# Steps 20 to 34 of a fused attention and ELU network with every engine's order written out and the weight conversion taken apart by engine

## The chip, the cores and the metric

The kernel runs on one core of one Trainium2 chip. The metric is the device time of one execution in microseconds, the median of several executions. The engines are named as in the profile: PE is TensorE, PEld its weight loads, DVE is VectorE, ACT ScalarE, POOL GpSimd, SP SyncE.

## The reference

A threshold attention over 8 sequences with 8 heads of 576 positions is followed by a two-layer network with an ELU between. The weights arrive as 64-bit floats. The reference, abridged:

```python
scores = scale * np.matmul(q, k.transpose(0, 1, 3, 2))
thresh = np.max(scores, axis=-1, keepdims=True) - tau
scores = np.where(scores >= thresh, scores, -1000000000.0)
attn = np.exp(scores - np.max(scores, axis=-1, keepdims=True))
attn = attn / (np.sum(attn, axis=-1, keepdims=True) + 1e-09)
x = np.matmul(attn, v)            # then (B, H, S, D) -> (B*S, H*D) = (4608, 512)
h = x @ w_in                      # (512, 2048)
g = np.where(h > 0.0, h, np.exp(np.minimum(h, 0.0)) - 1.0)
return g @ w_out                  # (2048, 512)
```

## The kernel before

The attention goes in 160 steps. Five steps make a pair of heads: four with two heads and 128 query rows, and one (called one-head here) with the last 64 rows of both. A step has scores on PE, a maximum over them on DVE, the bias and the threshold on POOL (`nb`, `th`), two exponentials on ACT, two masks with sums on DVE, a normalisation on POOL, and a turn of the weights, which PE does in steps 20 to 34 and DVE with DMA from 35 on. Units of the second network are put between: a unit is 8 matmuls of 128x256 or 4 of 128x512, and runs as two halves.

The double weights are turned to fp32 in 32 pieces of 128x512, 26 of them in steps 20 to 34. One piece, as it was:

```python
def convert_w():
    i = progress[1]
    ...
    top = wstage.tile([P, WN], U32, name="wtop", bufs=1)
    nc.vector.tensor_scalar(top, hi, 3, 0x3FFFFFFF, ALU.logical_shift_left, ALU.bitwise_and)      # L135
    nc.vector.scalar_tensor_tensor(top, hi, 0xC0000000, top, ALU.bitwise_and, ALU.bitwise_or)     # L136
    rest = lo.bitcast(I32)
    nc.scalar.mul(rest, lo, 2.0**-29)                                                              # L139
    top = top.bitcast(I32)
    nc.gpsimd.tensor_tensor(top, top, rest, ALU.add)                                               # L141
    mag = hi.bitcast(FP32)
    nc.scalar.activation(mag, mag, AF.Abs)                                                         # L144
    nc.vector.scalar_tensor_tensor(dst, mag, 1.125 * 2.0**-15, top.bitcast(FP32), ALU.is_ge, ALU.mult)  # L145
    load_w()
```

The loop of steps 20 to 34, whose order on the engines was left to the scheduler, and the quotas of the loop after it:

```python
for n in range(per_seq, SWITCH):          # 20 to 34
    pr, i = steps[n]
    ahead(pr, i)
    begin(pr, i, heads_of(i))             # scores, maximum, nb, th, exponentials
    convert_w()
    convert_w()
    finish(pr, i, heads_of(i))            # masks, normalisation
    turn(*steps[n - 1])
    behind(*steps[n - 2])                 # values
    due = min(due + rate, len(units))     # rate 1.4
    while due >= 1 and units:
        run_unit()
        due -= 1
...
# inside a unit of the first layer, and likewise of the second:
while progress[1] < 2 * KJ * (u // 4 + 1):
    convert_w()
...
QUOTA = ((2, 2), (2, 2), (2, 0), (2, 1), (2, 0))   # half units in each step of a pair, from step 35
```

## Time and profile before

| | before |
|---|---|
| device time, median of 4 | 1440.14 us (1438.64 to 1443.88) |
| first maximum with two heads, step 20 | at 105.8 us |
| step 20 to step 35, between their maxima | 159.1 us |
| step 35 to step 40 | 36.5 us |
| step 40 to the end of the span | 1134.6 us |

The last three rows are differences of start times of the maximum over the scores, which DVE takes once a step, so they cut the span at the same work in every kernel. A row of the timeline gives the start, the duration, the engine, the line, the operation, output and inputs, the shapes, and in brackets how long the engine had been idle and what ended that. The prediction shows the lines of before.

### The profile page before, as it was taken

How to read it: one execution, taken by the hardware profiler on the slowest of the kernel's cores; microseconds unless marked ns; L12 is line 12 of the kernel's file. 1: busy time of each engine (PE TensorE's matmuls, PEld its weight loads, DVE VectorE, ACT ScalarE, POOL GpSimd, SP SyncE). 2: the span in 40 equal slices, each digit the busy share in tenths (PEclk: the TensorE clock that was granted, in tenths of full speed). 3: DMA queues.
4: the chain of work that ended last, by engine and by line, in shares of the span. 5: the costliest groups of instructions: out<-in, count | busy, mean ns of one | idle time of the engine just before them, and what ended most of it. 6: DMA issues, size and time to landing. Idle time of an engine off the chain costs nothing.

```text
span 1436.0 us, 20455 instructions
## 1 busy us (share of the span) xinstructions
PE 1377.6 (96%) x6758; PEld 1023.8 (71%) x6758; DVE 949.1 (66%) x2070; ACT 451.2 (31%) x812; POOL 660.6 (46%) x1170
## 2 busy tenths in 40 slices
PE   6988788999999999999999999999999999999998
PEld 4555544647777777777777777777777777788887
DVE  6887665567677667766776767676777677563542
ACT  5665554323232222323232323232322222130220
POOL 4665554446544453536362635354444535151230
PEclk9999999999999999999999999999999999999999
DMA  4344443176667676767676767667676765100001
GB/s 95 78 92 113 111 125 93 43 196 191 188 171 207 178 191 173 193 186 190 178 192 186 189 180 193 185 183 201 180 199 174 191 189 166 62 1 15 15 1 30
DMA packets 298905, 205.45 MB, mean 143 GB/s; under 512 B 206384, under 2 KB 270384, under 8 KB 298800
## 3 DMA queue, kind: packets, MB, share of 16 engines
q1 hardware_dynamic: 298800, 204.15, 53.1%
q8 instruction: 54, 0.88, 0.2%
q14 instruction: 51, 0.42, 0.1%
HBM read 119.87 MB, written 84.21 MB: 142 GB/s over the span
## 4 chain that ended last, share of the span: by engine, by line
PE 82%; DVE 8%; POOL 4%; ACT 3%; issue 2%; DMA 1%; SPq 0%; POOLq 0%; DVEq 0%
PE ph L393 26%; PE po L500 24%; PE sc L220 12%; PE pv L347 8%; PE po L766 7%; DVE w L247 2%; PE pv L343 2%; PE po L465 2%; ACT e L235 2%; DVE mx L230 2%; POOL wtop L141 2%; PE rt L259 1%; POOL w L256 1%; DVE wtop L136 1%; POOL nb L231 1%
## 5 line engine op out<-in xcount | busy, mean ns | idle before, releaser
L393 PE MATMUL ph<-xt,w_in_sb 128*128 128x256 f32 x1792 | 409.3, 383 | 3.2 <-DVE w_in_sb L145 3.2
L393 PEld LDWEIGHTS ph<-xt,w_in_sb 128*128 128x128 f32 x1792 | 335.3, 190 | 70.2 <-issue 21.0
L235 ACT ACTIVATE e<-sc,nb,keep 128x576 f32<-128x576 f32 x288 | 227.8, 829 | 439.4 <-POOL nb L231 438.3
L230 DVE TENSOR_REDUCE mx<-sc 128x2 f32<-128x1152 f32 (+1 forms) x176 | 199.8, 1136 | 228.2 <-PE sc L220 228.0
L256 POOL TENSOR_SCALAR w<-w,rs 128x576 f32<-128x576 f32 x288 | 220.3, 775 | 223.3 <-DVE rs L250 216.6
L247 DVE SCALAR_TENSOR_TENSOR w<-sc,th,e 128x576 f32<-128x576 f32 x288 | 226.7, 815 | 78.0 <-ACT e L235 52.1
L220 PE MATMUL sc<-kT,qT 64*128 64x288 f32 x1024 | 180.4, 438 | 19.7 <-DVE w L247 9.6
L307 DVE STREAM_TRANSPOSE x<-w 128x512 f32<-128x512 f32 (+1 forms) x350 | 181.1, 567 | 0.9 <-POOL w L256 0.9
L231 POOL TENSOR_SCALAR nb<-mx,nkeep 128x2 f32<-128x2 f32 (+1 forms) x176 | 52.1, 296 | 263.4 <-DVE mx L230 256.5
L220 PEld LDWEIGHTS sc<-kT,qT 64*128 64x128 f32 x1024 | 99.3, 190 | 86.8 <-issue 53.5
L500 PE MATMUL po<-t,s 128*128 128x256 f32 x512 | 122.8, 386 | 4.5 <-DVE u L520 4.5
L500 PE MATMUL po<-w_out_sb,s 128*128 128x256 f32 x512 | 120.1, 384 | 0.0
L500 PEld LDWEIGHTS po<-t,s 128*128 128x128 f32 x512 | 94.6, 190 | 28.9 <-DVE u L520 8.9
L500 PEld LDWEIGHTS po<-w_out_sb,s 128*128 128x128 f32 x512 | 95.4, 190 | 19.7 <-issue 4.7
L401 ACT ACTIVATE g<-ph 128x512 f32<-128x512 f32 x112 | 66.9, 597 | 130.5 <-PE ph L393 130.5
L500 PE MATMUL po<-w_out_sb,g 128*128 128x256 f32 x448 | 103.2, 379 | 0.0
L404 POOL TENSOR_SCALAR g<-g 128x512 f32<-128x512 f32 x112 | 70.3, 627 | 67.4 <-ACT g L401 66.3
L500 PEld LDWEIGHTS po<-w_out_sb,g 128*128 128x128 f32 x448 | 85.1, 190 | 12.2
L408 DVE SCALAR_TENSOR_TENSOR g<-g,ph 128x512 f32<-128x512 f32 x112 | 75.0, 670 | 18.0 <-POOL g L404 17.9
L430 POOL TENSOR_TENSOR s<-g 128x256 f32<-128x256 f32 x112 | 82.6, 738 | 3.9 <-DVE g L810 3.9
L347 PE MATMUL pv<-wTb,vm 128*64 128x320 f32 x512 | 76.7, 439 | 0.0
L350 ACT COPY xt<-pv 128x256 f32<-128x256 f32 x64 | 23.8, 372 | 158.8 <-PE pv L347 158.8
(161 smaller groups left out, 1509.7 us busy)
## 6 DMA issues: line engine op xcount, KB each, us to landing
there<-x SPq DMA_DIRECT2D x500, 144.0 KB, 3.6
wTb<-there SPq DMA_DIRECT2D x75, 576.0 KB, 4.4
wTa<-there SPq DMA_DIRECT2D x50, 576.0 KB, 3.7
qm<-in_q_dram SPq DMA_DIRECT2D x128, 72.0 KB, 2.7
km<-in_k_dram SPq DMA_DIRECT2D x128, 72.0 KB, 3.7
vm<-in_v_dram SPq DMA_DIRECT2D x64, 128.0 KB, 2.5
wst<-in_moe_w_in_dram SPq DMA_DIRECT2D x16, 512.0 KB, 4.2
wst<-in_moe_w_out_dram SPq DMA_DIRECT2D x16, 512.0 KB, 3.7
```

The lines of the kernel that those rows point to most:

```text
L220: nc.tensor.matmul(scs[h][:, a, :HALF], qs[r], kT[r, k0 : k0 + HALF], start=True, stop=True)
L230: nc.vector.tensor_reduce(st["mx"][:, cs], src[:, :, :, :HALF], axis=AX.XY, op=ALU.max)
L235: nc.scalar.activation(e, st[h][:, :, :HALF], AF.Exp, bias=st["nb"][:, h : h + 1], scale=keep)
L247: nc.vector.scalar_tensor_tensor(wv, sc[:, :, :HALF], st["th"][:, h : h + 1], e, ALU.is_ge, ALU.mult, accum_out=sm[:, h : h + 1])
L256: nc.gpsimd.tensor_scalar(wv, wv, st["rs"][:, h : h + 1], 1.0, ALU.mult, ALU.mult)
L307: nc.vector.transpose(x[:, :, c0 : c0 + nc_], src.rearrange("p (c g n) -> p g c n", c=nc_, n=T))
L347: nc.tensor.matmul(pv[h * D : (h + 1) * D, g0 * T : g1 * T], vm[:, h, c], wT[:, g0:g1, h * (NC + 1) + c], start=False, stop=(c == NC - 1), ...
L393: nc.tensor.matmul(loc["ph"][:, k], w_in_sb[:, j, ft * P : (ft + 1) * P], xts[g][:, j, hf * CT : (hf + 1) * CT], start=(j == 0), stop=(j = ...
L408: nc.vector.scalar_tensor_tensor(loc["g"], loc["g"], 0.0, loc["h"], ALU.min, ALU.max)
L430: engines[k].tensor_tensor(out, x, y, op)
L500: nc.tensor.matmul(cur[c, place], lhs, rhs, start=(begins and u == 0), stop=(u == NU - 1), skip_group_check=True)
L766: nc.tensor.matmul(place, left[:, k], right[:, k], start=(begins and k == 0), stop=(k == 1), skip_group_check=True)
```

## The change

The intent is to keep DVE from standing inside each conversion. The five parts of a conversion become functions of their own and are laid at different places of a step; steps 20 to 34 get a written order on all engines; units start only when their weights are ready (`needs`); the weights of the first layer are converted in the order of their columns, and a unit of it takes two neighbouring column blocks (not in the cut below); the two output tiles of the second layer take turns, so that its weights are needed half as fast; and four half units more go into steps 35 to 39.

```diff
-    pieces = [(moe_w_in, ..., j, n) for n in (0, 2 * WN, WN, 3 * WN) for j in range(KJ)]
+    pieces = [(moe_w_in, ..., j, n) for n in range(0, DF, WN) for j in range(KJ)]
-        st = staged[i] = wstage.tile([P, WN, 2], U32, name="wst")
+        st = staged[i] = wstage.tile([P, WN, 2], U32, name="wst", bufs=4)
+    def convert_rest(i): ...   # ACT
+    def convert_top(i): ...    # DVE, two instructions; wtop with bufs=2
+    def convert_add(i): ...    # POOL
+    def convert_abs(i): ...    # ACT
+    def convert_end(i): ...    # DVE
...
-                units.extend((ffn2_plain, (c, i, p)) for i in range(2) for p in range(NFT // 4))
+                units.extend((ffn2_plain, (c, i, p)) for p in range(NFT // 4) for i in range(2))
...
+    SHARES = ((2, 1, 1), (1, 1, 0), (2, 1, 0), (1, 1, 0), (2, 1, 0))
+    with tc.manual_schedule():
+        for n in range(per_seq, SWITCH):
+            now = range(progress[1], min(progress[1] + 2, len(pieces)))
+            scores(*step, hs)
+            if valued: out_values = values(...)          # PE part only
+            for x in now[:1]: convert_top(x)
+            finish_units(carried, slice(0, 2))
+            for x in now[:1]: convert_add(x)
+            copies = parts[0]()
+            exponentials(*step, hs)                       # maximum, nb, th, exponentials
+            finish_units(carried, slice(2, None))
+            if valued: out_values(); copies()
+            for x in now[:1]: convert_abs(x)
+            after = ffn_halves(share[0])
+            for x in now[1:]: convert_top(x); convert_add(x); convert_abs(x)
+            ...                                           # turns, more halves
+            masks(*step, hs)
+            for x in now: convert_end(x)
+            finish_units(after + second, slice(2, None))  # ELU
+            normalize(*step, hs)
+            ...                                           # q, k, loads
+            for x in (the next two): convert_rest(x)
...
     QUOTA = ((2, 2), (2, 2), (2, 0), (2, 1), (2, 0))
+    FIRST = ((2, 2), (2, 2), (2, 2), (2, 2), (2, 1))      # for steps 35 to 39
```

(The loop is abridged: some `if`s stand on one line, and copies, shares and loads are cut.)

More of the change, by code (lines that the diff above doesn't have):

```diff
@@ L104, with load_w @@
     WN = 512
-    pieces = [(moe_w_in, w_in_sb[:, j, n : n + WN], j, n) for n in (0, 2 * WN, WN, 3 * WN) for j in range(KJ)]
+    pieces = [(moe_w_in, w_in_sb[:, j, n : n + WN], j, n) for n in range(0, DF, WN) for j in range(KJ)]
     pieces += [(moe_w_out, w_out_sb[:, f, n : n + WN], f, n) for f in range(NFT) for n in range(0, DM, WN)]
-    staged = {}
+    staged, tops = {}, {}
     progress = [0, 0]
-    def load_w():
+    def load_w(ahead=2):
         i = progress[0]
-        if i >= len(pieces) or i >= progress[1] + 2:
+        if i >= len(pieces) or i >= progress[1] + ahead:
             return
@@ L119, in load_w, with convert_rest, convert_top, convert_add @@
             return
-        st = staged[i] = wstage.tile([P, WN, 2], U32, name="wst")
+        st = staged[i] = wstage.tile([P, WN, 2], U32, name="wst", bufs=4)
         nc.sync.dma_start(st.rearrange("p n w -> p (n w)"), rows.bitcast(U32)[:, 2 * n : 2 * (n + WN)])
+    def convert_rest(i):
+        if i in staged:
+            lo = staged[i][:, :, 0]
+            nc.scalar.mul(lo.bitcast(I32), lo, 2.0**-29)
+    def convert_top(i):
+        if i in staged:
+            hi = staged[i][:, :, 1]
+            top = tops[i] = wstage.tile([P, WN], U32, name="wtop", bufs=2)
+            nc.vector.tensor_scalar(top, hi, 3, 0x3FFFFFFF, ALU.logical_shift_left, ALU.bitwise_and)
+            nc.vector.scalar_tensor_tensor(top, hi, 0xC0000000, top, ALU.bitwise_and, ALU.bitwise_or)
+    def convert_add(i):
+        if i in staged:
+            top = tops[i].bitcast(I32)
+            nc.gpsimd.tensor_tensor(top, top, staged[i][:, :, 0].bitcast(I32), ALU.add)
+    def convert_abs(i):
+        if i in staged:
+            mag = staged[i][:, :, 1].bitcast(FP32)
+            nc.scalar.activation(mag, mag, AF.Abs)
+    def convert_end(i):
+        progress[1] = i + 1
+        if i in staged:
+            mag, top = staged.pop(i)[:, :, 1].bitcast(FP32), tops.pop(i).bitcast(FP32)
+            nc.vector.scalar_tensor_tensor(pieces[i][1], mag, 1.125 * 2.0**-15, top, ALU.is_ge, ALU.mult)
     def convert_w():
@@ L126, in convert_w @@
             return
-        progress[1] += 1
-        if i not in staged:
-            load_w()
-            return
-        st, dst = staged.pop(i), pieces[i][1]
-        lo, hi = st[:, :, 0], st[:, :, 1]
-        top = wstage.tile([P, WN], U32, name="wtop", bufs=1)
-        nc.vector.tensor_scalar(top, hi, 3, 0x3FFFFFFF, ALU.logical_shift_left, ALU.bitwise_and)
-        nc.vector.scalar_tensor_tensor(top, hi, 0xC0000000, top, ALU.bitwise_and, ALU.bitwise_or)
-        rest = lo.bitcast(I32)
-        nc.scalar.mul(rest, lo, 2.0**-29)
-        top = top.bitcast(I32)
-        nc.gpsimd.tensor_tensor(top, top, rest, ALU.add)
-        mag = hi.bitcast(FP32)
-        nc.scalar.activation(mag, mag, AF.Abs)
-        nc.vector.scalar_tensor_tensor(dst, mag, 1.125 * 2.0**-15, top.bitcast(FP32), ALU.is_ge, ALU.mult)
+        for f in (convert_top, convert_rest, convert_add, convert_abs, convert_end):
+            f(i)
         load_w()
@@ L267, in turned_tile, with turn_parts @@
         return wTs[pr, min(i // 2, 1)], i % 2 * NT + (NT // 2 if i >= 2 else 0)
-    def turn(pr, i):
+    def turn_parts(pr, i):
         w = open_steps.pop((pr, i))["w"]
@@ L274, in to, with room @@
             nc.scalar.copy(wT[r, gs, cs].rearrange("p g c n -> p c g n"), src.rearrange("p c (g n) -> p c g n", n=T))
-        if i < NC:
-            for c0, c1 in ((0, NC), (NC + 1, NCH), (NC, NC + 1)):
-                rt = psum["t"].tile([P, NC, P], FP32, name="rt", tag="rt")
-                for c in range(c0, c1):
-                    transpose(rt[:, c - c0], w[:, c * P : (c + 1) * P])
-                to(slice(g0, g0 + NT), slice(c0, c1), rt[:, : c1 - c0])
-        else:
-            ga, gb = slice(0, 2), slice(3 * NT - 2, 3 * NT)
-            rt = psum["t"].tile([P, NC, P], FP32, name="rt", tag="rt")
+        def room():
+            return psum["t"].tile([P, NC, P], FP32, name="rt", tag="rt")
@@ L286, in turn, with chunks, tails @@
+        def chunks(c0, c1):
+            rt = room()
+            for c in range(c0, c1):
+                transpose(rt[:, c - c0], w[:, c * P : (c + 1) * P])
+            return lambda: to(slice(g0, g0 + NT), slice(c0, c1), rt[:, : c1 - c0])
+        ga, gb = slice(0, 2), slice(3 * NT - 2, 3 * NT)
+        def tails():
+            rt = room()
             for c in range(NC):
                 transpose(rt[:, c], w[:, c * P : (c + 1) * P])
-            to(ga, slice(0, NC), rt[:, :, :TAIL])
-            to(gb, slice(NC + 1, NCH), rt[:, :, TAIL:])
@@ L290, in turn, with copies, common @@
-            rt = psum["t"].tile([P, NC, P], FP32, name="rt", tag="rt")
+            def copies():
+                to(ga, slice(0, NC), rt[:, :, :TAIL])
+                to(gb, slice(NC + 1, NCH), rt[:, :, TAIL:])
+            return copies
+        def common():
+            rt = room()
             transpose(rt[:TAIL, 0], w[:, MAIN:S])
             transpose(rt[:, 1], w[:, S - P : S])
-            cs = slice(NC, NC + 1)
-            to(ga, cs, rt[:TAIL, :1, :TAIL], slice(0, TAIL))
-            to(ga, cs, rt[TAIL:, 1:2, :TAIL], slice(TAIL, P))
@@ L298, in turn, with copies @@
-            to(gb, cs, rt[:, 1:2, TAIL:])
+            def copies():
+                cs = slice(NC, NC + 1)
+                to(ga, cs, rt[:TAIL, :1, :TAIL], slice(0, TAIL))
+                to(ga, cs, rt[TAIL:, 1:2, :TAIL], slice(TAIL, P))
+                to(gb, cs, rt[:, 1:2, TAIL:])
+            return copies
+        if i < NC:
+            return [lambda: chunks(0, NC), lambda: chunks(NC + 1, NCH), lambda: chunks(NC, NC + 1)]
+        return [tails, common]
+    def turn(pr, i):
+        for part in turn_parts(pr, i):
+            part()()
@@ L348, in values, with values_out @@
                                  start=False, stop=(c == NC - 1), skip_group_check=True)
-        q0 = TAIL * part
+        return lambda: values_out(pr, part, pv)
+    def values_out(pr, part, pv):
+        b, j = divmod(pr, NPAIR)
+        q0, n = TAIL * part, (3 if part else 2) * NT * T
         nc.scalar.copy(xts[b][:, j, part * 2 * P : (part + 1) * 2 * P], pv[:, q0 : q0 + 2 * P])
@@ L383, in ffn1 @@
         loc = {}
+        fts = (u, u + NU) if c >= PLAIN else (2 * u, 2 * u + 1)
         def part(k):
-            ft = u + k * NU
-            if not late:
-                while progress[1] < 2 * KJ * (u // 4 + 1):
-                    convert_w()
+            ft = fts[k]
             if k == 0:
@@ L398, in exp @@
                 gs[c] = [gpool.tile([P, NU, 2, 2, P], FP32, name="g")]
-            loc["g"] = hidden(c, u, 1).rearrange("p u j i t -> p (u j i t)")
-            loc["h"] = loc["ph"].rearrange("p k t -> p (k t)")
-            nc.scalar.activation(loc["g"], loc["h"], AF.Exp)
+            g = hidden(c, u, 1)[:, 0] if c >= PLAIN else hidden(c, 2 * u % NU, 2)[:, :, 2 * u // NU]
+            loc["g"] = g.rearrange("p a i t -> p a (i t)")
+            nc.scalar.activation(loc["g"], loc["ph"], AF.Exp)
         def minus():
@@ L406, in elu @@
         def elu():
-            nc.vector.scalar_tensor_tensor(loc["g"], loc["g"], 0.0, loc["h"], ALU.min, ALU.max)
+            nc.vector.scalar_tensor_tensor(loc["g"], loc["g"], 0.0, loc["ph"], ALU.min, ALU.max)
             if u % 2 and c >= PLAIN:
@@ L458, in run @@
         def run(k):
-            if not late:
-                while progress[1] < len(pieces):
-                    convert_w()
             if part == 0 and k == 0:
@@ L474, in done @@
                     weight_sums(u, True)
-        return [lambda: run(0), lambda: run(1)], (done, lambda: None, lambda: None) if 4 * part + 4 == NFT else ()
+        no = lambda: None
+        return [lambda: run(0), lambda: run(1)], (done, no, no) if 4 * part + 4 == NFT else (no, no, no)
     ORDER = ((("g", 0, 0), ("w", 0, 0), "X", True), (("g", 1, 1), ("t", 2), "Z", True), (("g", 1, 0), ("w", 1, 0), "X", False),
@@ L553, in behind @@
         if i in (1, NB - 1):
-            values(pr, 0 if i == 1 else 1)
+            values(pr, 0 if i == 1 else 1)()
         if i == NB - 1 and (pr + 1) % NPAIR == 0 and pr + 1 < NP:
@@ L562, with needs @@
     pending = deque()
+    def needs(f, a):
+        if f is ffn1:
+            return KJ * (2 * a[1] // 4 + 1) if a[0] == 0 else KJ * KJ
+        return KJ * KJ + 4 * (a[2] + 1) if f is ffn2_plain else len(pieces)
     def ffn_halves(n):
@@ L567, in ffn_halves @@
             if not pending:
+                if needs(*units[0]) > progress[1]:
+                    break
                 f, a = units.popleft()
@@ L581, in finish_units @@
                 post()
-    def run_unit():
-        finish_units(ffn_halves(2), slice(0, None))
     def begin(*step):
@@ L632 @@
     SWITCH = (NPAIR + 3) * NB
-    due = 0.0
-    rate = 1.4
-    for n in range(per_seq, SWITCH):
-        pr, i = steps[n]
-        ahead(pr, i)
-        begin(pr, i, heads_of(i))
-        convert_w()
-        convert_w()
-        finish(pr, i, heads_of(i))
-        turn(*steps[n - 1])
-        behind(*steps[n - 2])
-        due = min(due + rate, len(units))
-        while due >= 1 and units:
-            run_unit()
-            due -= 1
-    turn(*steps[SWITCH - 1])
-    behind(*steps[SWITCH - 2])
@@ L650 @@
-    behind(*steps[SWITCH - 1])
+    SHARES = ((2, 1, 1), (1, 1, 0), (2, 1, 0), (1, 1, 0), (2, 1, 0))
+    ACT, OTHER, ALL = slice(0, 1), slice(1, None), slice(0, None)
+    with tc.manual_schedule():
+        carried = []
+        for _ in range(2):
+            load_w(4)
+        for n in range(per_seq, SWITCH):
+            pr, i = step = steps[n]
+            hs = heads_of(i)
+            now = range(progress[1], min(progress[1] + 2, len(pieces)))
+            if n == per_seq:
+                for x in now:
+                    convert_rest(x)
+            for _ in now:
+                load_w(4)
+            scores(*step, hs)
+            valued = steps[n - 2][1] in (1, NB - 1)
+            if valued:
+                out_values = values(steps[n - 2][0], 0 if steps[n - 2][1] == 1 else 1)
+            parts = turn_parts(*steps[n - 1])
+            for x in now[:1]:
+                convert_top(x)
+            finish_units(carried, slice(0, 2))
+            for x in now[:1]:
+                convert_add(x)
+            copies = parts[0]()
+            if not valued:
+                copies()
+            exponentials(*step, hs)
+            finish_units(carried, slice(2, None))
+            if valued:
+                out_values()
+                copies()
+            for x in now[:1]:
+                convert_abs(x)
+            share = SHARES[n % NB]
+            after = ffn_halves(share[0])
+            finish_units(after, ACT)
+            for x in now[1:]:
+                convert_top(x)
+                convert_add(x)
+                convert_abs(x)
+            parts[1]()()
+            second = ffn_halves(share[1])
+            finish_units(second, ACT)
+            if len(parts) > 2:
+                parts[2]()()
+            carried = ffn_halves(share[2])
+            masks(*step, hs)
+            finish_units(after + second, slice(1, 2))
+            for x in now:
+                convert_end(x)
+            finish_units(after + second, slice(2, None))
+            normalize(*step, hs)
+            if i in (2, 3):
+                (prep_q if i == 2 else prep_k)(pr + 1)
+                (copy_q if i == 2 else copy_k)(pr + 1)
+            if i in (3, 4):
+                load(pr + 2, ("qm",) if i == 3 else ("km",))
+            if i == 3:
+                load(pr + 1, ("v",))
+            if steps[n - 2] == (NPAIR - 1, NB - 1):
+                push_ffn(0)
+            for x in range(progress[1], min(progress[1] + 2, progress[0])):
+                convert_rest(x)
+        finish_units(carried, ALL)
+        turn(*steps[SWITCH - 1])
+        finish_units(ffn_halves(len(pending)), ALL)
+        behind(*steps[SWITCH - 2])
+        behind(*steps[SWITCH - 1])
@@ L698 @@
             step = (*steps[n], heads_of(steps[n][1])) if n < len(steps) else None
+            quota = (FIRST if n < SWITCH + NB else QUOTA)[n % NB]
             if SWITCH + 1 < n <= len(steps) + 1:
@@ L714 @@
                 turn_squares(*steps[n - 1])
-            after = ffn_halves(QUOTA[n % NB][0])
+            after = ffn_halves(quota[0])
             if step:
@@ L731 @@
                 load(pr + 1, ("v",))
-            after = ffn_halves(QUOTA[n % NB][1])
+            after = ffn_halves(quota[1])
         finish_units(after, slice(0, None))
```

## The prediction

> **What bounds the kernel now.** I read the page first, then a table of stretches, the DVE's row of events, the waits of the conversion's last instruction, and the chain of waits. The page says that TensorE is 96% busy over the span, so only the places where it isn't can give anything:
>
> ```profile
> PE   6988788999999999999999999999999999999998
> DVE  6887665567677667766776767676777677563542
> ...
> PEclk9999999999999999999999999999999999999999
> ```
>
> One digit is 35.9 us. From the eighth slice on PE stays at 9; the 8s and the 7 of slices 2 to 7 cover the steps that the change rewrites (slice 1 and most of 2 are before them). I located the steps by the maximum over the scores, one per step (L230 on DVE; a 128x1 row is the last, one-head step of a pair). Step 20 is the first with two heads at once:
>
> ```profile
> 105.82 1.35 DVE L230 TENSOR_REDUCE mx<-sc 128x2 f32<-128x1152 f32 x1
> ...
> 157.81 1.34 DVE L230 TENSOR_REDUCE mx<-sc 128x2 f32<-128x1152 f32 x1
> 179.76 1.35 DVE L230 TENSOR_REDUCE mx<-sc 128x2 f32<-128x1152 f32 x1
> ...
> 217.03 1.35 DVE L230 TENSOR_REDUCE mx<-sc 128x2 f32<-128x1152 f32 x1
> 233.88 1.35 DVE L230 TENSOR_REDUCE mx<-sc 128x2 f32<-128x1152 f32 x1
> ...
> 253.35 0.76 DVE L230 TENSOR_REDUCE mx<-sc 128x1 f32<-128x576 f32 x1 [2.40 <-PE sc L220]
> 264.96 1.36 DVE L230 TENSOR_REDUCE mx<-sc 128x2 f32<-128x1152 f32 x1 [5.12 <-PE sc L220]
> ```
>
> Step 20 to step 35 takes 264.96 - 105.82 = 159.1 us, 10.6 us a step. It is uneven: steps 26 and 31 take 22.0 and 16.9 us. Those are where a unit of the second network asks for more converted weights (the `while progress[1] < ...` loops), so that several conversions run one behind the other. The stretches, columns PE, PEld, DVE, ACT, POOL busy, then granted clock, DMA share, GB/s:
>
> ```profile
> 102.20:263.60 161.40, 132.69 (x608) 80.90 (x608) 102.14 (x192) 83.68 (x165) 82.73 (x104) 0.96 0.40 103
> 263.60:300.20 36.60, 34.98 (x156) 23.70 (x156) 24.75 (x52) 10.04 (x14) 25.32 (x37) 1.00 0.42 107
> ...
> 337.80:375.50 37.70, 37.70 (x196) 28.79 (x194) 26.93 (x58) 11.96 (x20) 25.81 (x45) 1.00 0.71 190
> ```
>
> In steps 20 to 34 no engine is full: PE 82%, DVE 63%. So a chain of waits across engines is the bound. In steady state (last line) PE is. The DVE waits inside each conversion:
>
> ```profile
> its engine sat idle before it (us, times) until:
>   POOL wtop L141: 22.4, 19
>   ACT wst L144: 3.6, 2
> ```
>
> That is L145, the conversion's last instruction, between 102 and 264 us: DVE makes `top` (L135, L136), then stands until GpSimd has added and ScalarE has taken the magnitude, 26.0 us in 26 pieces. Around it, in the order of DVE:
>
> ```profile
> 225.63 0.69 DVE L145 SCALAR_TENSOR_TENSOR w_out_sb<-wst,wtop 128x512 f32<-128x512 f32 x1 [1.77 <-POOL wtop L141]
> 226.35 0.78 DVE L135 TENSOR_SCALAR wtop<-wst 128x512 uint32<-128x512 uint32 x1
> 227.16 1.11 DVE L136 SCALAR_TENSOR_TENSOR wtop<-wst,wtop 128x512 uint32<-128x512 uint32 x1
> 229.83 0.69 DVE L145 SCALAR_TENSOR_TENSOR w_out_sb<-wst,wtop 128x512 f32<-128x512 f32 x1 [1.56 <-POOL wtop L141]
> ```
>
> About 4 us a piece where 1.7 us is work; `wtop` has one buffer, so nothing of the next piece can start. The chain of waits over this stretch agrees: its largest entry is POOL wtop L141 with 14.4%, or 23 us.
>
> **What the Trainium skill says.** "Perfetto Trace Analysis", section Identifying the Most-Contended Engine, says that busy time of matmuls overstates TensorE. So I count its work below instead: 117 us in 161, where the page's way of counting gives 133. "SBUF — State Buffer", in its list of practical consequences below the port table, says that a DVE instruction with two SBUF inputs contends with a GpSimd instruction that reads SBUF, and that the order of issue decides who blocks. The trace agrees: L136 took 0.69 us in most cases, 1.11 in the row at 227.16. "TensorE: Matmul & The Clock Gate", section What's actually happening, says that the array's clock is lowered when it has been idle. Here the granted clock is 0.96 over the stretch (0.71 in 156 to 165 us) and 1.00 afterwards, so some of the time is that of slower matmuls.
>
> **The change, part by part.** It removes no arithmetic: the same 26 conversions, units and turns. TensorE's work by its own spacing in the chain: a unit is 3.55 us (16 records of L393 or 8 of L465; a half 1.78), scores 1.17 a step, turns 1.0, the values of a pair 5.5. A pair of five steps has 4 x 1.17 + 1.1 + 4.7 + 5.5 = 16 us without units, three pairs 48.
>
> *Units.* Before: 14 steps at 1.4 give 19 units, 67.5 us, with attention 115 to 117: some 45 us of 161 are not matmul work. After: I followed the quotas with `needs` (two pieces a step, ten ready at step 22); the break bites at steps 30 and 32, and I count 34 half units, 17 units, 60 us: PE has 108 us to do. The two units less are the four halves more in steps 35 to 39.
>
> *Conversion.* Its instructions stay; its 26 us of DVE waits go, as both pieces' `top`, `add`, `abs` and `end` lie apart with other DVE work between, with two `wtop` and four `wst` buffers. The 3.9 us wait on a weight transfer that the chain has at 173 us goes too.
>
> *The new bound* is DVE's loop, in its written order. From one maximum to the mask takes 3.46 us, whatever lies between, as the mask begins only after both exponentials:
>
> ```profile
> 288.08 1.34 DVE L230 TENSOR_REDUCE mx<-sc 128x2 f32<-128x1152 f32 x1
> ...
> 289.89 1.55 ACT L235 ACTIVATE e<-sc,nb,keep 128x576 f32<-128x576 f32 x2 [4.22 <-POOL nb L231]
> ...
> 291.54 0.82 DVE L247 SCALAR_TENSOR_TENSOR w<-sc,th,e 128x576 f32<-128x576 f32 x1 [0.71 <-ACT e L235]
> ```
>
> It covers the second piece's `top` (1.1 us by start to start). Then two masks, sum and reciprocal, 1.89 (L247 at 284.94 to the next transpose at 286.83); two ends, 2 x 0.62 = 1.25; ELU, 0.6 in nine of thirteen steps, 0.4; the q and k transposes, 0.68 in two of five, 0.27; the first piece's `top`, 1.1; for the shared port I choose 0.3. Sum 8.67 us. A one-head step: 2.1 to its mask (253.35 to 255.45) + 0.6, as the 1.29 us addition stands before `nb` on GpSimd + 1.14 + 1.25 + 0.4 + 1.1 + 0.3 = 6.9. Thirteen converting steps: 11 x 8.67 + 2 x 6.9 = 109.2. Step 33 is PE's: 2.2 + values 2.3 + two halves 3.55 = 8.0. Step 34 to the scores of 35 is PE's too, in order: turns 1.0, three halves 5.3, turn of 34 0.9, the last half 1.8, values 3.2, and the copies that free the banks 0.8: 13.0. Sum 130 us, against 263.60 - 105.82 = 157.8: **28 us less**.
>
> *Steps 35 to 39*: two are full of PE work already (four halves and scores, 8.27). The other three become 8.27, 8.27 and, with values, 8.75, from 6.6, 6.6 and 7.0: **5 us more**. From step 40 on the backlog is the same (19 + 7.5 units, 17 + 9.5) and PE is full, so nothing else moves. Net -23; a slightly earlier first maximum, perhaps 1 us. 1441.1 - 24 = 1417.
>
> **Rivals.** (a) *PE becomes the bound*: waits hide perfectly, and the stretch takes 108 us of PE work plus some 10 at its ends, 118: 40 - 5 = 35 us, 1406. For it: the quotas sum to 7 units a pair, 41 us, about my DVE loop; against it: DVE has 102 us of its own work and the 3.46 us chain. (b) *A new wait takes the old one's place*: in-order queues make ScalarE or GpSimd late (values copied out before `abs`, the addition before `nb`), or scores come late behind half units; 1.5 us a step more is 20 us, which leaves 1436. For it: ACT has 84 us and POOL 83 in the stretch already, and the one score tile (L220 waits for DVE w L247) gives scores under 2 us of slack. (c) *Only the bursts go*: steps 26 and 31 lose their 17 us of excess over the mean, the added 5 is paid: 1429.
>
> **Range and chances.** 2% is 28.8 us, so 1412 is the line. An error of 0.5 us in the loop is 7 us, and I think it likelier too short than too long. Range 1403 to 1433; faster by over 2% 0.31, within 2% 0.66, slower 0.03.
>
> **What would show it.** Right: maxima 20 to 35 near 131 us apart at 8 to 9 us a step, no step of 17 us; L145's wait on L141 below 4 us; mask waits on ACT e as the largest DVE wait; PE's clock 1.00 there; 35 to 40 near 42 us. Wrong: large waits of PE sc on DVE w with the maximum waiting for sc (PE-bound), GpSimd nb waiting behind its additions, or any change after step 40.

## The result, and the profile after

| | before | after |
|---|---|---|
| device time, median of 4 | 1440.14 us | 1422.12 us (1419.89 to 1422.82) |
| ratio | | 0.9868 (0.9845 to 0.9892) |
| first maximum of step 20 | 105.8 | 106.9 |
| step 20 to step 35 | 159.1 | 134.4 (-24.7) |
| step 35 to step 40 | 36.5 | 41.6 (+5.1) |
| step 40 to the end | 1134.6 | 1135.2 (+0.6) |

A ratio is the mean time of one kernel's fast runs over the mean of the other's of the same rounds, so it is not quite the ratio of the medians. The change is 1.3% faster, which counts as "within 2%". The profiled spans, 1436.0 and 1418.1 us, differ by 17.9 us, and the rows of the table add up to it: 1.1 - 24.7 + 5.1 + 0.6 = -17.9. The first maximum varies by itself: a second profile of the changed kernel has it at 110.3 us, so I compare from there on.

The page of the changed kernel, share of each 35.5 us in tenths:

```profile
PE   6897989999999999999999999999999999999998
...
PEclk9999999999999999999999999999999999999999
```

Nines begin one slice earlier than before. The maxima of steps 20, 26 to 28, 31, 32, 34 and 35, as DVE has them:

```profile
106.92 1.36 DVE L246 TENSOR_REDUCE mx<-sc 128x2 f32<-128x1152 f32 x1 [2.47 <-PE sc L236]
...
160.15 1.34 DVE L246 TENSOR_REDUCE mx<-sc 128x2 f32<-128x1152 f32 x1
170.57 1.34 DVE L246 TENSOR_REDUCE mx<-sc 128x2 f32<-128x1152 f32 x1
179.68 1.35 DVE L246 TENSOR_REDUCE mx<-sc 128x2 f32<-128x1152 f32 x1
...
204.15 1.34 DVE L246 TENSOR_REDUCE mx<-sc 128x2 f32<-128x1152 f32 x1
212.91 1.34 DVE L246 TENSOR_REDUCE mx<-sc 128x2 f32<-128x1152 f32 x1
...
227.60 0.76 DVE L246 TENSOR_REDUCE mx<-sc 128x1 f32<-128x576 f32 x1 [1.00 <-PE sc L236]
241.30 1.36 DVE L246 TENSOR_REDUCE mx<-sc 128x2 f32<-128x1152 f32 x1 [3.04 <-PE sc L236]
```

Steps 26 and 31, 22.0 and 16.9 us long before, take 10.4 and 8.8. The five rows in the middle show no idle time in front: DVE came to the maximum straight from other work, and the scores lay ready. Inside a step of the changed kernel, in the order of DVE:

```profile
151.26 1.35 DVE L246 TENSOR_REDUCE mx<-sc 128x2 f32<-128x1152 f32 x1
152.53 0.62 DVE L135 TENSOR_SCALAR wtop<-wst 128x512 uint32<-128x512 uint32 x1
153.19 0.69 DVE L136 SCALAR_TENSOR_TENSOR wtop<-wst,wtop 128x512 uint32<-128x512 uint32 x1
154.98 0.82 DVE L263 SCALAR_TENSOR_TENSOR w<-sc,th,e 128x576 f32<-128x576 f32 x1 [1.11 <-ACT e L251]
...
156.87 1.27 DVE L154 SCALAR_TENSOR_TENSOR w_out_sb<-wst,wtop 128x512 f32<-128x512 f32 x2
```

L154 is the conversion's last instruction, L145 of before. Both pieces pass without a wait. The one idle time left is the 1.11 us before the mask (L263), which begins 3.72 us after the maximum. The waits from 103 to 240 us (engine and line, waiting for what: us in total, times, longest) say the same:

```profile
DVE w L263 <- ACT e L251: 16.4, 15, 2.1
...
DVE w_in_sb L154 <- ACT wst L147: 0.4, 1, 0.4
```

The 26.0 us of waits inside conversions have become 0.4. The waits for exponentials are now DVE's largest. They are not new: before, L247 waited 14.3 us for them over its stretch.

### The profile page after: what moved, and what is told of

Its sections match the earlier page's. It is cut to its first block, busy times and chain, and to the rows that moved or that the text cites. A ratio compares the mean times of both kernels' runs of the same rounds, so it can differ in the third digit from the quotient of the medians.

```text
span 1418.1 us, 20448 instructions
## 1 busy us (share of the span) xinstructions
PE 1373.6 (97%) x6758; PEld 1024.1 (72%) x6758; DVE 950.5 (67%) x2070; ACT 449.2 (32%) x812; POOL 669.4 (47%) x1170
## 4 chain that ended last, share of the span: by engine, by line
PE 84%; DVE 8%; ACT 3%; POOL 2%; issue 2%; SPq 0%; DMA 0%; DVEq 0%; POOLq 0%
PE ph L434 26%; PE po L539 24%; PE sc L236 12%; PE pv L386 9%; PE po L868 7%; DVE w L263 3%; ACT e L251 3%; PE po L503 2%; PE pv L382 2%; DVE mx L246 2%; PE rt L275 1%; POOL wtop L142 1%; DVE wtop L136 1%; POOL nb L247 1%; DVE wtop L135 1%
## 5 line engine op out<-in xcount | busy, mean ns | idle before, releaser
L272 POOL TENSOR_SCALAR w<-w,rs 128x576 f32<-128x576 f32 x288 | 224.3, 789 | 224.7 <-DVE rs L266 216.8
L263 DVE SCALAR_TENSOR_TENSOR w<-sc,th,e 128x576 f32<-128x576 f32 x288 | 226.2, 815 | 78.5 <-ACT e L251 54.9
L236 PE MATMUL sc<-kT,qT 64*128 64x288 f32 x1024 | 181.1, 439 | 22.4 <-DVE w L263 12.0
L247 POOL TENSOR_SCALAR nb<-mx,nkeep 128x2 f32<-128x2 f32 (+1 forms) x176 | 51.2, 291 | 261.7 <-DVE mx L246 253.8
L449 DVE SCALAR_TENSOR_TENSOR g<-g,ph 128x512 f32<-128x512 f32 x112 | 74.8, 669 | 18.2 <-POOL g L445 18.1
```

What stands on the lines that cost most here:

```text
L236: nc.tensor.matmul(scs[h][:, a, :HALF], qs[r], kT[r, k0 : k0 + HALF], start=True, stop=True)
L263: nc.vector.scalar_tensor_tensor(wv, sc[:, :, :HALF], st["th"][:, h : h + 1], e, ALU.is_ge, ALU.mult, accum_out=sm[:, h : h + 1])
L272: nc.gpsimd.tensor_scalar(wv, wv, st["rs"][:, h : h + 1], 1.0, ALU.mult, ALU.mult)
L449: nc.vector.scalar_tensor_tensor(loc["g"], loc["g"], 0.0, loc["ph"], ALU.min, ALU.max)
```

## The experiments

"Steps 20 to 33" is the time between those maxima, 113.5 and 113.0 us in the two profiles of the changed kernel.

### The control

No edit.

> The changed kernel again, as the control of this call: ratio to before about 0.987, some 1421 us, steps 20 to 33 about 113 us between their maxima.

Measured: 1422.71 us, ratio 0.9869 (0.9845 to 0.9894). The steps repeat within some hundredths of a microsecond, but for step 21 (9.19 and 8.75 us). So step times of one profile each can be compared to about half a microsecond, while whole spans differ by up to 4 us in the first stretch before step 20.

### One more instruction on DVE, at two places

```diff
+            if again:   # the result is the same: the two bit operations can be repeated
+                nc.vector.scalar_tensor_tensor(top, hi, 0xC0000000, top, ALU.bitwise_and, ALU.bitwise_or)
 # dup_first:  convert_top(x, True) for the first piece, ahead of the maximum
 # dup_second: convert_top(x, True) for the second piece, between maximum and mask
```

> The second instruction that makes `top` is run twice for the first piece of a step, which lies just ahead of the maximum on DVE. Theory (DVE's loop is the bound, and this place is on it): 13 x 0.62 = +8 us against the changed kernel, all of it in steps 20 to 32. Rival 1 (TensorE is the bound in these steps): +0 to 2 us. Rival 2 (the sum of DVE's work counts, wherever it lies): +8 us, as the run dup_second.

> The same instruction run twice for the second piece, which lies between the maximum and the mask, where DVE waits 1.1 us a step for the exponentials. Theory (the chain maximum, nb, two exponentials, mask is the floor, and what DVE does meanwhile is free): +0 to 2 us, and DVE's wait for the exponentials falls from 16 to about 8 us. Rival 1 (TensorE): +0. Rival 2 (DVE's sum): +8 us.

Measured: dup_first 1429.78 us (0.9927, 0.9897 to 0.9957), dup_second 1420.97 us (0.9867, 0.9843 to 0.9891). The same instruction costs 7 to 8 us at one place and nothing at the other. In the trace of dup_first steps 20 to 33 take 121.5 us, 8 to 8.5 more; in dup_second the two-head steps are those of the control to 0.02 us and only the one-head steps, whose gap is shorter, are 0.5 us longer. DVE's wait for the exponentials, in dup_second between 100 and 226 us:

```profile
DVE w L265 <- ACT e L253: 6.2, 12, 2.1
```

The longest of these, 2.1 us, is that of step 33, which has no conversion. In steps 20 to 32 DVE waits 4.0 us for the exponentials, where it waits 12.8 us in the control. The instruction filled the wait. So DVE's loop is the bound in these steps, not the sum of its work and not TensorE: what counts is whether an instruction lies beside the chain of maximum, `nb`, exponentials and mask, or on the path.

### The order on GpSimd

```diff
-            for x in now[:1]:
-                convert_add(x)
...
             exponentials(*step, hs)
+            for x in now[:1]:
+                convert_add(x)
```

> On GpSimd the addition of the first piece is put behind nb and th, so that they need not wait for it. Theory (the addition lengthens the chain from the maximum to the mask from the 3.46 us before to 3.7 to 4.0 us): maximum to mask back to about 3.5 us, -3 to -7 us in all. Rival (GpSimd is off the path, or the additions then come too late for the ends of the conversions): 0, or L154 waiting for L142.

Measured: 1421.63 us, 0.9865 (0.9838 to 0.9891): no gain, a miss. The chain did become shorter: the mask begins 3.51 or 3.52 us after the maximum in ten of the eleven converting two-head steps (3.72 in most of them before the edit), and 2.2 instead of 3.0 in the one-head steps. That is some 3.6 us in all. But steps 20 to 33 still take 113.2 us. DVE's own instructions became longer, between 104 and 225 us in both traces: the mean of L136 rose from 0.81 to 0.84 us (26 of them), of L154 from 0.68 and 0.75 to 0.75 and 0.85 (16 and 11), of the sum's small instruction L265 from 0.17 to 0.28 (11), some 4.4 us together. L135 fell by 3.5 us, but mostly in the second piece, which lies beside the chain. So what the chain gave, the longer instructions took. That these are collisions with GpSimd, whose additions now come later, is argued from the means and not isolated.

### Both first parts behind the maximum

```diff
-            for x in now[:1]: convert_top(x)
             finish_units(carried, slice(0, 2))
-            for x in now[:1]: convert_add(x)
...
             exponentials(*step, hs)
+            for x in now[:1]: convert_top(x); convert_add(x)
```

> The first piece's `top` and addition move from ahead of the maximum to behind it and nb/th, so that both pieces' `top` lie beside the chain from maximum to mask. Theory (DVE's loop): 13 x 1.1 us leave the loop, less what of the 2.2 us does not fit into the wait of 2.2 us (3.46 - 1.27): -6 to -12 us against the changed kernel, until TensorE's 108 us bind. Rival (TensorE is the bound already): within 2 us. Rival (the additions come too late): L154 waits for L142, gain under 4 us.

Measured: 1422.69 us, 0.9874 (0.9856 to 0.9892): a miss of the same kind, and here it can be seen in the rows. DVE and GpSimd of tops_after, one row of each timeline:

```profile
152.76 1.82 DVE L136 SCALAR_TENSOR_TENSOR wtop<-wst,wtop 128x512 uint32<-128x512 uint32 x1
```

```profile
152.74 1.29 POOL L142 TENSOR_TENSOR wtop<-wtop,wst 128x512 int32<-128x512 int32 x1
```

GpSimd's addition of the first piece began 0.02 us before DVE's second `top` instruction, that of the second piece, and ended at 154.03. DVE ended at 154.58, 0.55 us later; alone this instruction takes 0.69 us. All eleven converting two-head steps show the same, with 1.81 to 1.83 us. That is the block that the Trainium skill, "SBUF — State Buffer", states in its practical consequences for a DVE instruction with two SBUF inputs against a GpSimd instruction that reads SBUF. The mean of L136 rose to 1.17 us, and the mask began 4.5 us after the maximum in place of 3.7. In addition the maximum waited for scores in five of the steps 21 to 32, 4.9 us in all, where the control waits for none: TensorE was reached in some steps. The order of the change, with the first addition beside the maximum, which reads PSUM, avoids this collision.

### One instruction into the wait

```diff
-            for x in now: convert_end(x)
+            for x in now[:1]: convert_end(x)
+            held = now[1:]            # done in the next step, right after exponentials(...)
```

(with five `wst` and three `wtop` buffers, loading one piece further ahead)

> The second piece's last instruction on DVE moves from behind the mask to the next step's wait between maximum and mask, where DVE waits 1.0 us a step (one staged and one wtop buffer more). Theory (that wait is free room): 12 x 0.62 = 7 us leave the loop, less what collides with GpSimd there: -2 to -6 us against the changed kernel, 1416 to 1420. Rival (as in nb_first and tops_after, the collision with GpSimd's addition takes it all, or TensorE's scores come late): within 1.5 us.

Measured: 1418.24 us, 0.9847 (0.9831 to 0.9863), inside the forecast by the median. But the control has 0.9869, and the intervals overlap. It was run at another time. By the trace, from the maximum of step 20 to that of step 39 it takes 165.6 us, against 167.2 and 166.7 in the two profiles of the change, so only 1.1 to 1.6 us less; its first maximum is at 107.1 us, and that of the control at 110.3 us by chance. Of the 7 us that leave the path most come back: the mask begins 4.14 us after the maximum in the step at 150 us (3.72 in the control). There `nb` took 0.95 us in place of 0.44, while the moved instruction ran on DVE for the first part of it; in all twelve steps with a moved instruction it took 0.80 to 0.96 us. That the moved instruction is what lengthens it is read from the rows, not isolated.

### The conversions whole, in the written order

```diff
-            for x in now[:1]: convert_top(x)  # and the other parts at their places
...
-            for x in now:
-                convert_end(x)
+            for x in now:
+                for f in (convert_top, convert_rest, convert_add, convert_abs, convert_end):
+                    f(x)
```

> The written order stays, but each conversion runs whole again, all five parts one behind the other where the ends were. Theory (taking the conversion apart is what pays): DVE waits some 1.6 us or more in each of 26 pieces and the chain of a piece is about 4 us, so +30 to +45 us against the changed kernel, slower than before or as slow (1440 to 1465). Rival (the end of the bursts is what pays, one piece at a time does no harm): +0 to 10 us.

Measured: 1489.99 us, 1.0347 (1.0331 to 1.0363), slower than both kernels and by more than I expected. Steps 20 to 33 take 182.6 us, 14 us a step. DVE's waits in whole from 105 to 290 us:

```profile
DVE w_out_sb L154 <- POOL wtop L142: 39.5, 16, 6.4
...
DVE w_in_sb L154 <- POOL wtop L142: 22.8, 10, 5.5
```

That is 62.3 us in 26 pieces, 2.4 each, where I had taken 1.6. The written order alone is much worse than the scheduler's; it pays only together with the conversion taken apart.

### The buffers alone

```diff
-        if i >= len(pieces) or i >= progress[1] + 2:
+        if i >= len(pieces) or i >= progress[1] + 4:
-        ... name="wst")                # and wtop with bufs=1
+        ... name="wst", bufs=4)        # and wtop with bufs=2
```

(in the kernel before)

> The kernel before with nothing but the buffers of the change (four staged pieces loaded ahead, two wtop). Theory (order, not room, made DVE wait inside the conversion): within 5 us of before. Rival (room alone was the matter): more than half of the gain of the change, -10 us or better.

Measured: 1443.1 us, 1.0020 (1.0000 to 1.0041). Nothing gained. But the reading is not as simple as my theory had it: with the room, L145's waits for GpSimd did fall, from 22.4 to 9.0 us, and the steps 20 to 33 still took 139.1 us (136.0 before), step 26 alone 27.9 us. In that run the maximum waited 15.3 us for scores up to step 34, against 4.8 us before. So taking away DVE's waits inside conversions was not enough here. I read it so that the bursts, which hold the scores of the next step behind units that need weights, must go with them; no run took away the bursts alone, and none tested `needs` or the alternating output tiles by themselves.

### TensorE's bound, with a wrong result

```diff
+        bare[0] = True   # in steps 20 to 32 top, rest, add and abs are left out; L154 remains
```

> Wrong result on purpose: in steps 20 to 32 the conversions lose all but their last instruction on DVE, so the weights are wrong. It shows how far TensorE's bound lies below. Theory (DVE's loop binds by a little only): DVE loses 1.1 us a step ahead of the maximum, GpSimd 2.6 and ScalarE 2.7; then TensorE binds with 108 us of work and about 10 at the ends: steps 20 to 35 in 118 to 124 us against 134, -10 to -16 us in all. Rival (DVE and its waits hold the steps much longer than TensorE): -20 us or more. Rival (TensorE binds already): within 3 us.

Measured: 1412.79 us, 0.9808 (0.9786 to 0.9829). Steps 20 to 33 take 102.9 us, 10.1 less than the control's 113.0, and the maximum waits 8.1 us for scores in steps 21 to 32, where the control waits for none. So even with most of the conversion free of charge only 10 us are to be had in these steps; TensorE is close behind DVE's loop.

### The quota of steps 35 to 39

```diff
 # old_quota, in the changed kernel: 15 half units
-            quota = (FIRST if n < SWITCH + NB else QUOTA)[n % NB]
+            quota = QUOTA[n % NB]
 # first_17, in the changed kernel: 17 half units
-    FIRST = ((2, 2), (2, 2), (2, 2), (2, 2), (2, 1))
+    FIRST = ((2, 2), (2, 2), (2, 2), (2, 1), (2, 0))
 # before_first: FIRST of 19 half units in the kernel before
```

> Steps 35 to 39 with the old quota of 15 half units. Theory (units are only moved, TensorE is full later): steps 35 to 40 take 5 us less, the four half units (7.1 us) come later where TensorE is full, so +2 us in all. Rival (the quota is a part of the gain of its own): +5 to 7 us. Rival (it costs): -5 us.

> Steps 35 to 39 with 17 half units, midway between 15 (1432 us) and 19 (1422 us). Theory (which unit meets which step of a pair in steady state decides): the tail is 3.5 us longer and steps 35 to 40 about 2.5 shorter, as sums of 1.78 us halves; the pairs from step 40 on take either 76.2 us for two as in the changed kernel or up to 77.1, not something midway in each. Rival (a plain price of the backlog): 1427, midway in everything.

> The kernel before with the new quota of 19 half units in steps 35 to 39 alone. Theory (the quota only makes up for the two units that steps 20 to 34 do less, and keeps the steady state in step): here it takes units out of the tail, +5 us in steps 35 to 40 and up to -7 in the tail, and shifts the steady state: -3 to +10 us against before, no gain of 1%. Rival (the quota is half of the change's gain by itself): -8 to -10 us.

| | device us | ratio to before | 35 to 40 | two pairs in steady state | last one-head maximum to end |
|---|---|---|---|---|---|
| before (15 half units) | 1440 | | 36.5 | 76.2 | 227.9 |
| change (19) | 1422.12 | 0.9868 | 41.6 | 76.2 | 227.9 |
| old_quota (15) | 1432.02 | 0.9944 (0.9923 to 0.9964) | 36.6 | 77.1 | 234.8 |
| first_17 (17) | 1413.43 | 0.9809 (0.9791 to 0.9828) | 38.1 | 75.5 | 231.3 |
| before_first (19) | 1456.71 | 1.0105 (1.0086 to 1.0125) | 41.6 | 77.4 | 226.5 |

This is the largest miss, in both directions. I had expected +2 us for old_quota, 76.2 to 77.1 us for two pairs in first_17, and at most +10 us for before_first. Measured were +9.9, -8.7 and +16.2 us. In the three forms of the changed kernel the last column follows the backlog as expected: two half units are 3.5 us, four are 7. In before_first it doesn't, with 1.4 us: the 64 half units of the first sequence were used up early, and steps 40 to 44 ran three half units fewer than before (34.6 us against 37.6). The column before the last decides: the time of two pairs in steps 40 to 159 changes with the quota, 77.1, 75.5 and 76.2 us for 15, 17 and 19 half units, and that is paid about twelve times. Counted from the matmuls, before and the change have both done 53 half units by step 40, and both take 76.2 us; old_quota has done 49 and first_17 51. The stretch from 400 to 1180 us in the changed kernel, in first_17, in old_quota and in before_first (columns as in the prediction):

```profile
400.00:1180.00 780.00, 775.56 (x3924) 587.69 (x3922) 545.32 (x1185) 222.11 (x370) 369.72 (x700) 1.00 0.69 187
```

```profile
400.00:1180.00 780.00, 780.00 (x3965) 593.46 (x3964) 550.90 (x1196) 222.39 (x374) 373.33 (x707) 1.00 0.70 188
```

```profile
400.00:1180.00 780.00, 768.10 (x3886) 580.90 (x3886) 539.31 (x1172) 218.13 (x365) 364.43 (x690) 1.00 0.70 185
```

```profile
400.00:1180.00 780.00, 761.60 (x3870) 579.68 (x3868) 536.81 (x1167) 213.32 (x362) 357.15 (x683) 1.00 0.69 184
```

PE, the first figure behind the comma, is idle for 4.4, 0, 11.9 and 18.4 us. What PE waited for in that stretch, in the changed kernel, in old_quota and in before_first; in first_17 no such line exists:

```profile
PE po L539 <- DVE u L559: 4.1, 10, 0.4
```

```profile
PE po L539 <- DVE g L449: 11.0, 10, 1.1
```

```profile
PE po L500 <- DVE g L408: 18.4, 10, 1.8
```

Ten times in 780 us, once in two pairs, a second-layer product needs an ELU of DVE (L449, L408) or a bank that DVE empties (L559). In the chain of old_quota that DVE instruction stands behind the step's maximum, exponentials, masks, sum and reciprocal. Where the backlog places the product there, PE waits; with 17 half units it doesn't. Per two pairs PE is idle for 0.4, 1.2 and 1.8 us with 19 half units, in old_quota and in before_first; that is most of the 0.7, 1.6 and 1.9 us by which two pairs take longer than in first_17, and the rest is open. The quota of five steps thus sets the phase of the units against the steps for the remaining 120. For first_17 the parts add up, against the control from step 35 on: 3.5 us less in steps 35 to 40, some 8.1 less in steady state, 3.5 more in the tail, together 8.1; the profiled spans are 1412.8 and 1420.9, with the first maximum at 110.3 us in both.

So first_17 beats both kernels: 0.9809 of before, 1.9% faster (whether by over 2% is unclear from the interval), correct, with one line of the change altered. It was not run together with end_late, and no quota besides 15, 17 and 19 was tried.

## Why the prediction was right or wrong

The prediction said 1417 us, range 1403 to 1433, and "within 2%" with 0.66. Measured were 1422.12 us and 1.3% faster, so it was right, with 23 to 24 us forecast and 18 found.

- **What bounds the kernel before: half right.** The uneven steps and the DVE waits inside conversions are there, and the change removed them (26.0 to 0.4 us). But I reckoned the waits inside conversions as the loss. before_bufs took away most of them and gained nothing. That the bursts, which I named only as rival (c), had to go with them is argued from before_bufs and not shown by a run of its own; how the 24.7 us divide between waits and bursts stays open. whole shows the other half: the written order without the conversion apart is slower than before.
- **The new bound: right, and shown.** DVE's loop binds; dup_first and dup_second differ by 9 us for the same instruction. The masks' wait on the exponentials is DVE's largest, as forecast.
- **The size of the loop: the term that was too small.** Thirteen converting steps were to take 109.2 us and took 113.5. The two-head steps took 8.97 us in the mean (8.67 forecast), the one-head steps 7.97 and 6.85 (6.9). From the maximum to the mask I took 3.46 us from a step without conversions; it is 3.72 in most, as `nb` stands behind the addition on GpSimd (nb_first brought it to 3.51): 0.26 in nine of eleven steps and 0.57 in step 26, some 3 us. I had put this term into the one-head steps only, where it measured 3.0 and not 2.7. The rest is in single steps such as 26 (10.4 us, with 1.14 us in which DVE waits for the ELU's input from GpSimd). The 0.3 us for the shared port were not isolated by a run. The trace shows some 0.2 of them: seven of the 26 L136 took 0.76 to 1.12 us in place of 0.69, 2.5 us in all, and each ended 0.54 us after an L272 of GpSimd that was running when it began.
- **Steps 33 to 35: right within 1.5 us.** 8.0 for step 33 measured 7.2. From the maximum of 34 to the scores of 35 I had 13.0; they began at 239.94, 12.3 us after it. TensorE was busy in all of that but the 0.79 us before the scores, by the trace.
- **Units: right.** The traces of steps 20 to 34 hold nine units of the first layer and eight of the second, 17.
- **Steps 35 to 40: right,** 41.6 us against "near 42" and +5.1 against +5.
- **"Nothing else moves" from step 40 on: right, for an incomplete reason.** 1134.6 and 1135.2 us. I argued that PE is full and that the backlog is the same. The second is true and is what matters; the first is not quite, and reckoning with the old quota on this ground I was wrong by 8 us (old_quota). Without its four half units the change would have been worth 0.6%, not 1.3%.
- **PE's clock "1.00 there": wrong.** It is 0.98 from 103 to 240 us, against 0.96 before in its stretch.
- **A first maximum 1 us earlier: not found;** it was 1.1 us later, within what two profiles of the same kernel differ by.

Of the rivals, (a) with PE as the bound lay 10 us further off, by ends_only; (b) came true in small, as 0.3 us a step; (c) would have left 1429 us, more than was measured.

## What to carry to other kernels

When an engine waits in its own queue for two others, lay the parts of the work apart and put independent work between. But look at which engine pairs then run at once, since here three rearrangements of the same parts gained 0 to 2 us by their traces. Here an instruction was free beside the chain that set the loop, as long as it fitted into the wait, and cost its full length on the path; doubling one instruction at each of two places told which was which. When a backlog is shifted between stages, time the steady state too: how many half units were done before it set whether TensorE was idle in each of the following pairs, and against the 19 of the change, two half units fewer took 9 us off and four fewer added 10, each half of what the whole change gave.

## What the Trainium skill lacked or had wrong

- "Perfetto Trace Analysis", section Optimization Strategy, gives a lack of SBUF or PSUM room as what a bubble that repeats can mean. Here a bubble that repeats once in two pairs, 0.4 us with 19 half units and 1.1 us with 15, went away with 17 of them in five steps far ahead of it, no buffer changed: PE was busy in 775.56, 768.10 and 780.00 of 780 us. The page isn't wrong: with 19 the wait is for a PSUM bank (L559), but with 15 it is for an ELU (L449). No page that I read has this phase of queued work against a loop.
- "SBUF — State Buffer", practical consequences, was confirmed, not wrong: L136 took 1.82 us when GpSimd's addition had begun 0.02 us before it. The other order shows in the traces too: `th`, 128x2 elements, took 0.27 us in the kernel before in a step without conversions (at 283 us) and 0.70 us in the mean in the changed kernel. In the step at 151 us it began 0.08 us after DVE's L136 and ended 0.13 us after it.
